# Two more units of a convolution moved to channel-major jobs, with neighbouring blocks sharing a job

## The chip, the cores and the metric

The kernel runs on one core of a Trainium2 chip. The metric is the device time of one execution in microseconds (us). A core has five engines that run side by side and wait for one another by semaphores: TensorE (PE, matrix products; its weight loads are listed as PEld), VectorE (DVE), ScalarE (ACT), GpSimd (POOL) and SyncE (SP, which here only issues DMAs). DMAs are issued from SP's queue or from POOL's and carried out by 16 DMA engines. Each engine works through its own instructions in program order.

## The reference

A causal convolution with one softmaxed filter of 7 taps for each of 8 groups of 24 channels, and then a gated feed-forward block, both over 8 sequences of 4096 tokens with 192 channels:

```python
w = softmax(weight)                      # 8 groups x 7 taps
x_pad = concatenate([zeros((B, 6, D)), x], axis=1)
out = einsum('hk,bskhg->bshg', w, windows of x_pad)   # 24 channels of a group share the 7 taps
x = out.reshape(32768, 192)
g = x @ w_gate                           # 192 x 1536
silu = g * (1.0 / (1.0 + exp(-g)))
val = x @ w_val
return (silu * val) @ w_out              # 1536 x 192
```

## The kernel before

**Tiling.** The 32768 tokens are 64 blocks of 512 (`TB`), four blocks to a unit (`UT` = 2048 tokens, 16 units, two to a sequence). The feed-forward part walks over the blocks; the 1536 inner features are 12 chunks of 128, so a block has 12 steps, a unit 48 (`ustep`), the kernel 768. The main loop at line 892 runs over steps n; b is the block, j the chunk, u the unit, ls the step in the unit.

**A step.** `gate_val` issues six matmuls of 64 x 128 weights on 512 columns (line 772), three channel tiles k for gate and val each, in pairs that run side by side in two halves of the PE array. ACT makes silu of the gate (line 781), DVE multiplies it with val (line 783). PSUM has three buffers each for gate and val. At j = 1, 4, 7 and 10 a `slot` follows, with the down projection's matmuls (line 798), and after the last of them the copies and the DMA of a block's output (lines 856 to 860).

**The input of a block** is three tiles of 128 channels x 512 tokens in fp16: channels 0 to 127, 64 to 191, and 128 to 191 with 0 to 63 (gate reads one half of a tile, val the other). There are two ways to make them:

- *On PE.* Units 0 (by a variant of its own for its four blocks), 1, 3, 7 and 11. x is loaded token-major by a DMA from POOL (`load_x`), doubled by SP (`dup_x`), multiplied with a band matrix on PE in two halves (`conv_half`, at ls 10 and 22 of the unit before), copied out of PSUM by ACT and DVE, completed by a copy on POOL (`conv_dup`), stored to DRAM by nine DMAs (`conv_out`) and read back by DMA transposes (`fetch`), three to a block.
- *Channel-major.* The units in `POOLED` (line 53): 2, 4, 5, 6, 8, 9, 10, 12 to 15. `cast_x` copies a unit of x to DRAM in fp16 (a DMA from POOL, line 590); `turn_x` reads it back transposed (line 605), so that channels lie on partitions and a tap is a shift along the tokens. There are two such tiles for each block, channels 0 to 127 (`x01`) and 64 to 191 (`x12`). Channels 128 to 191 fill only half the partitions, so those of two blocks share a tile: `join_x` (line 609) moves one block's 64 rows to the free half of another's. A unit then has six jobs (`conv_job`): four "block" jobs for channels 0 to 127, two "pair" jobs for 128 to 191. A job is, in order: two products on ACT (line 680; tap 0 into `total`, tap 3 into `part`), two multiply-adds on DVE (line 655, taps 1 and 2), and on POOL one add of `part` and, for taps 4, 5 and 6, a product (line 645) and an add (line 630) each. `total` has five buffers. The last add writes `pxc0` of the block, or `y2` of the pair. `place` then builds the other two tiles with four DMAs from SP (line 704).

**What sets the order.** `planned(v)` writes down the step of each piece for a channel-major unit v whose first step is s0 = 48 v: the cast at s0 - 112, the ten transposes and joins from s0 - 105, two steps apart, and the jobs into the lists at s0 - 89. Unit 2 has times of its own. `pooled_work` runs in each step: at j = 1, 7 and 10 it takes one DVE piece and one ACT piece off their lists (unless a `conv_half` or an early convolution runs in this step), which makes 12 turns in a unit, as many as a unit has pieces. POOL's seven instructions of a job are written when its ACT and DVE pieces are. `place` for block i is written when both its jobs are, at least 18 steps later (14 in unit 2), and not before s0 + 12 i - 16. All these instructions go to the queue of their engine in the order written, so a DMA that waits in SP's queue holds up those behind it, and a cast stands in POOL's queue behind the jobs written before it.

Of the kernel before, what the change touches and what calls it, by code (L numbers as in the profile page):

```python
# [10 lines left out]
def kernel(  # L11
# [9 lines left out]
    nc = tc.nc  # L21
# [13 lines left out]
    P = 128  # L35
    Q = 64
# [13 lines left out]
    ER = ((0, 3), (3, 5))  # L50
    XW = 2 * EG * EO
    NU = NT // UT
    POOLED = (2, 4, 5, 6, 8, 9, 10, 12, 13, 14, 15)
    upb = S // UT
    n_blocks = NT // TB
    n_steps = n_blocks * NCH
# [16 lines left out]
    def seq(i):  # L73

        e = i.ins.engine
        if e in last_on:
            tc.add_manual_dep(i.ins, last_on[e].name, NOSYNC, reason="order")
        last_on[e] = i.ins
        return i
# [106 lines left out]
    def small(name, shape, dt=fp32):  # L186
        return wpool.tile(shape, dt, tag=name, name=name)
# [106 lines left out]
    tap = small("tap", [P, 2 * H], fp16)  # L294
# [249 lines left out]
    x12 = {}  # L544
    y2 = {}
    taps = {}
# [29 lines left out]
    def cast_x(u):  # L576
        rows = XP + UT
        xs[u] = dpool.tile([rows, D], fp16, tag="xs", name="xs")
        flat = xs[u].rearrange("t d -> (t d)")
        skip = XP if u % upb == 0 else 0  # L580
        if skip:
            seq(
                nc.sync.dma_start(
                    out=flat[0 : XP * D].rearrange("(a n) -> a n", n=P),
                    in_=fill[0 : XP * D // P, :],
                )
            )
        n = (rows - skip) * D // P
        seq(
            nc.gpsimd.dma_start(  # L590
                out=flat[skip * D : rows * D].rearrange("(a n) -> a n", n=n),
                in_=bass.AP(
                    tensor=x_flat.tensor,
                    offset=(u * UT - XP + skip) * D,
                    ap=[[n, P], [1, n]],
                ),
            )
        )

    def turn_x(u, i, at):  # L600
        rows = xs[u][TB * i : TB * i + TB + XP]
        tiles = (x01, x12)[at // Q]
        tag = f"x{at // Q}"
        t = cpool.tile([P, TB + XP], fp16, tag=tag, name=tag, bufs=8)
        seq(nc.sync.dma_start_transpose(out=t, in_=rows[:, at : at + P]))
        tiles[u, i] = t

    def join_x(u, i):
        seq(nc.sync.dma_start(out=x12[u, i + 2][0:Q], in_=x12[u, i][Q:P]))

    FIRST, ON_DVE, ON_ACT, ON_POOL = 0, (1, 2), (3,), (4, 5, 6)
    act_steps = []
# [5 lines left out]
    def conv_job(u, what, i):  # L618
        index = n_jobs[0]
        n_jobs[0] += 1  # L620
        job = {"dve": len(ON_DVE), "act": len(ON_ACT), "parts": []}
        at = XP - pad

        def shifted(k):
            return job["src"][:, at + k : at + k + TB]

        def add(part, k):
            total = job["total"]
            seq(
                nc.gpsimd.tensor_tensor(  # L630
                    job["dst"] if k == K - 1 else total, total, part, op=ALU.add
                )
            )

        def proceed():
            if job["dve"]:
                return
            while job["parts"]:
                add(*job["parts"].pop(0))
            if job["act"]:  # L640
                return
            for k in ON_POOL:
                part = cpool.tile([P, TB], fp32, tag="piece", name="piece", bufs=2)
                seq(
                    nc.gpsimd.tensor_scalar(  # L645
                        part, shifted(k), scalar1=job["tap"][:, k : k + 1],
                        scalar2=1.0, op0=ALU.mult, op1=ALU.mult,
                    )
                )
                add(part, k)  # L650
            finished[u, what, i] = step_now[0]

        def dve_step(k):
            seq(
                nc.vector.scalar_tensor_tensor(  # L655
                    job["total"], shifted(k), job["tap"][:, k : k + 1], job["total"],
                    op0=ALU.mult, op1=ALU.add,
                )
            )
            job["dve"] -= 1  # L660
            proceed()

        def act_step(k):
            if k == FIRST:
                if what == "pair":
                    y2[u, i] = cpool.tile([P, TB], fp16, tag="y2", name="y2", bufs=4)
                    job.update(dst=y2[u, i], src=x12[u, i + 2], tap=taps["c2"])
                else:
                    t = cpool.tile([P, XW], fp16, tag="pxc0", name="pxc0", bufs=8)
                    xc[UB * u + i] = [t]  # L670
                    job.update(dst=t[:, 0:TB], src=x01[u, i], tap=taps["c01"])
                part = job["total"] = cpool.tile(
                    [P, TB], fp32, tag="total", name="total", bufs=5
                )
                dve_steps.extend((index, lambda k=k: dve_step(k)) for k in ON_DVE)
            else:
                part = cpool.tile([P, TB], fp32, tag="part", name="part", bufs=6)
                job["parts"].append((part, k))
            seq(
                nc.scalar.activation(  # L680
                    part, shifted(k), AF.Copy, scale=job["tap"][:, k : k + 1]
                )
            )
            if k != FIRST:
                job["act"] -= 1
                proceed()

        act_steps.extend((index, lambda k=k: act_step(k)) for k in (FIRST, *ON_ACT))

    def place(u, i):  # L690
        b = UB * u + i
        for k in (1, 2):
            xc[b].append(
                cpool.tile([P, XW], fp16, tag=f"pxc{k}", name=f"pxc{k}", bufs=4)
            )
        t0, t1, t2 = xc[b]
        y = y2[u, i % 2][Q * (i // 2) : Q * (i // 2) + Q, :]
        for dst, src in (
            (t1[0:Q, 0:TB], t0[Q:P, 0:TB]),
            (t1[Q:P, 0:TB], y),  # L700
            (t2[0:Q, 0:TB], y),
            (t2[Q:P, 0:TB], t0[0:Q, 0:TB]),
        ):
            seq(nc.sync.dma_start(out=dst, in_=src))  # L704

    def pooled(u):
        return u in POOLED

# [2 lines left out]

    def queue_jobs(u):
        for job in (
            ("block", 0), ("pair", 0), ("block", 1), ("pair", 1),
            ("block", 2), ("block", 3),
        ):
            conv_job(u, *job)
        placing.extend((u, i) for i in range(UB))

    def planned(v):  # L720
        s0 = ustep * v
        turns = (
            (0, 0), (0, Q), (2, Q), None, (1, 0), (1, Q), (3, Q), None, (2, 0), (3, 0)
        )
        if v == 2:
            cast, jobs = 21, 55
            times = (36, 36, 36, 38, 39, 39, 39, 41, 43, 43)
        else:
            cast, jobs = s0 - 112, s0 - 89
            times = range(cast + 7, cast + 27, 2)  # L730
        plan.setdefault(cast, []).append(lambda: cast_x(v))
        for m, turn in enumerate(turns):
            if turn:
                todo = lambda turn=turn: turn_x(v, *turn)
            else:
                todo = lambda i=m // 4: join_x(v, i)
            plan.setdefault(times[m], []).append(todo)
        plan.setdefault(jobs, []).append(lambda: queue_jobs(v))

    def pooled_work(n, j, busy):  # L740
        step_now[0] = n
        if not busy:
            ready = dve_steps[0][0] if dve_steps else None
            ahead = act_steps[0][0] if act_steps else n_jobs[0]
            if j in (1, 7, 10) and ready is not None:
                dve_steps.pop(0)[1]()
            if j in (1, 7, 10) and act_steps and (ready is None or ahead < ready + 3):
                act_steps.pop(0)[1]()
        while placing:
            u, i = placing[0]  # L750
            need = (u, "block", i), (u, "pair", i % 2)
            if not all(job in finished for job in need):
                break
            done = max(finished[job] for job in need)
            if n < max(done + (14 if u == 2 else 18), ustep * u + NCH * i - 16):
                break
            placing.pop(0)
            place(u, i)
# [129 lines left out]
    make_band()  # L888
    for v in POOLED:
        planned(v)  # L890

    for n in range(n_steps):
        b, j = divmod(n, NCH)
        u, ls = divmod(n, ustep)
# [31 lines left out]
        if n == 37:  # L926
            make_channel_taps()
        pooled_work(n, j, work is not None)
        if u + 1 < NU and not pooled(u + 1):
            if ls == at[0]:  # L930
# [62 lines left out]
```

## Time and profile before

| what | us |
|---|---|
| median of 3 runs (lowest, highest) | 784.47 (784.04, 785.72) |
| the profiled execution, whole | 786.03 |
| its span in the profile | 784.3 |
| PE busy | 774.7 |
| weight loads busy | 631.6 |
| DVE busy | 675.1 |
| ACT busy | 584.7 |
| POOL busy | 551.1 |

Three groups of instructions make up nearly all of POOL's time: 264 adds of line 630, of 1.32 to 1.37 us each, and 198 products of line 645 of 0.83. POOL's busy share in 40 equal slices of the span (a digit is tenths, 9 is 90% or more) shows where it works:

```profile
POOL 9100797699999990089999996029999999996000
```

Its three long stretches belong to the jobs of units 4 to 6, 8 to 10 and 12 to 15; the stretch of unit 2 is the shorter one ahead of them. Matmuls overlap, so a busy PE is not PE at its peak. Idle time of an engine that nobody waits for costs nothing; what counts is which wait ends last at a place where PE stands still.

### The profile page before, as it was taken

How to read it: one execution, taken by the hardware profiler on the slowest of the kernel's cores; microseconds unless marked ns; L12 is line 12 of the kernel's file. 1: busy time of each engine (PE TensorE's matmuls, PEld its weight loads, DVE VectorE, ACT ScalarE, POOL GpSimd, SP SyncE). 2: the span in 40 equal slices, each digit the busy share in tenths (PEclk: the TensorE clock that was granted, in tenths of full speed). 3: DMA queues.
4: the chain of work that ended last, by engine and by line, in shares of the span. 5: the costliest groups of instructions: out<-in, count | busy, mean ns of one | idle time of the engine just before them, and what ended most of it. 6: DMA issues, size and time to landing. Idle time of an engine off the chain costs nothing.

```text
span 784.3 us, 27860 instructions
## 1 busy us (share of the span) xinstructions
PE 774.7 (99%) x11307; PEld 631.6 (81%) x11307; DVE 675.1 (86%) x1018; ACT 584.7 (75%) x999; POOL 551.1 (70%) x523
## 2 busy tenths in 40 slices
PE   8999998999999999999999999999999999999997
PEld 5666675688888888778888888868989988888886
DVE  6686996999999987799999997789999999997775
ACT  6576885788788766787787776687787787876664
POOL 9100797699999990089999996029999999996000
PEclk9999998999999999999999999999999999999999
DMA  9949753675551296585364239557635255221211
GB/s 140 179 116 144 167 104 95 125 104 117 111 124 45 60 166 113 113 141 101 101 114 93 69 70 175 120 129 106 130 80 125 76 100 109 69 62 42 69 56 42
DMA packets 154470, 82.37 MB, mean 105 GB/s; under 512 B 98110, under 2 KB 153798, under 8 KB 153798
## 3 DMA queue, kind: packets, MB, share of 16 engines
q1 hardware_dynamic: 136422, 64.26, 37.4%
q0 software_dynamic: 17920, 16.34, 14.5%
q8 instruction: 88, 1.44, 0.8%
q14 instruction: 40, 0.33, 0.1%
HBM read 32.68 MB, written 38.34 MB: 91 GB/s over the span
## 4 chain that ended last, share of the span: by engine, by line
PE 96%; POOL 2%; ACT 0%; DVE 0%; DMA 0%; issue 0%; SPq 0%; POOLq 0%
PE val L772 36%; PE acc L798 31%; PE gate L772 27%; POOL total L630 1%; PE warm L873 1%; POOL piece L645 1%; PE cv L476 1%; PE turn L445 0%; PE cv L387 0%; PE acc L819 0%; DVE h L783 0%; DMA pxc<-pxc 0%; SPq L704 0%; POOL y L630 0%; ACT sig L781 0%
## 5 line engine op out<-in xcount | busy, mean ns | idle before, releaser
L781 ACT ACTIVATE sig<-gate 128x512 f16<-128x512 f32 x768 | 458.6, 597 | 181.9 <-PE gate L772 122.4
L783 DVE TENSOR_TENSOR h<-sig,val 128x512 f16<-128x512 f16 x768 | 502.5, 685 | 98.4 <-PE gate L772 65.0
L772 PEld LDWEIGHTS <-w 64*128 64x128 f16 x4608 | 362.4, 110 | 111.5 <-issue 6.8
L772 PE MATMUL gate<-pxc,w 64*128 64x512 f16 x1584 | 373.4, 377 | 2.3 <-DMA pxc<-pxc 2.2
L772 PE MATMUL val<-pxc,w 64*128 64x512 f16 x1584 | 373.0, 377 | 0.1
L798 PE MATMUL acc<-wo,h 64*128 64x192 f16 x6096 | 327.3, 243 | 0.6 <-issue 0.5
L798 PEld LDWEIGHTS <-h 64*128 64x128 f16 x6096 | 301.5, 94 | 27.5 <-issue 2.9
L630 POOL TENSOR_TENSOR total<-total,piece 128x512 f32<-128x512 f32 x132 | 179.1, 1357 | 11.0
L772 PE MATMUL gate<-xc,w 64*128 64x512 f16 x720 | 169.7, 376 | 0.0
L772 PE MATMUL val<-xc,w 64*128 64x512 f16 x720 | 169.6, 376 | 0.1
L645 POOL TENSOR_SCALAR piece<-x,both_taps 128x512 f32<-128x512 f16 x198 | 164.2, 829 | 0.0
L655 DVE SCALAR_TENSOR_TENSOR total<-x,both_taps,total 128x512 f32<-128x512 f16 x132 | 138.7, 1051 | 0.0
L630 POOL TENSOR_TENSOR total<-total,part 128x512 f32<-128x512 f32 x66 | 90.4, 1369 | 59.1 <-DVE total L655 58.1
L630 POOL TENSOR_TENSOR pxc<-total,piece 128x512 f16<-128x512 f32 x44 | 58.2, 1322 | 3.7
L504 POOL COPY tm<-tm 128x1280 f16<-128x1280 f16 x4 | 5.0, 1250 | 67.0 <-DVE tm L493 67.0
L680 ACT ACTIVATE part<-x,both_taps 128x512 f32<-128x512 f16 x66 | 47.1, 714 | 0.0
L680 ACT ACTIVATE total<-x,both_taps 128x512 f32<-128x512 f16 x66 | 47.1, 714 | 0.0
L857 DVE COPY o_sb<-acc 128x384 f32<-128x384 f32 x63 | 34.6, 549 | 0.0
L630 POOL TENSOR_TENSOR y<-total,piece 128x512 f16<-128x512 f32 x22 | 29.5, 1341 | 1.8
L856 ACT COPY o_sb<-acc 128x384 f32<-128x384 f32 x63 | 30.3, 481 | 0.1
L98 POOL DMA_DIRECT2D x<-in_x_dram x10 | 8.7, 885 | 24.4 <-ACT sig L781 24.4
L493 ACT CAST tm<-cv 128x480 f16<-128x480 f32 x16 | 8.2, 562 | 5.8 <-PE cv L476 5.8
(67 smaller groups left out, 85.9 us busy)
## 6 DMA issues: line engine op xcount, KB each, us to landing
out_dram<-o_sb SPq DMA_DIRECT2D x63, 384.0 KB
pxc<-pxc SPq DMA_DIRECT2D x88, 64.0 KB
pxc<-y SPq DMA_DIRECT2D x88, 64.0 KB
xs<-in_x_dram POOLq DMA_DIRECT2D x7, 768.0 KB, 6.9
x<-in_x_dram POOLq DMA_DIRECT2D x10, 480.0 KB, 9.3
scr<-tm SPq DMA_DIRECT2D x28, 130.0 KB
xs<-in_x_dram POOLq DMA_DIRECT2D x4, 774.0 KB, 8.9
x<-x SPq DMA_DIRECT2D x6, 480.0 KB
```

What stands on the lines that cost most here:

```text
L98: nc.gpsimd.dma_start(out=t[p0 + i0 : p0 + i1, w0 - at : w1 - at, :], in_=bass.AP(tensor=x_flat.tensor, offset=(t0 + size * w0 - pad + i0) ...
L493: eng(tm[u][:, NG * r : NG * r + NG, 2 * grp * hp : 2 * grp * hp + 2 * grp].rearrange("p g (t e) -> p g t e", t=2), banks[r][:, 0 : 2 * w] ...
L630: nc.gpsimd.tensor_tensor(job["dst"] if k == K - 1 else total, total, part, op=ALU.add)
L645: nc.gpsimd.tensor_scalar(part, shifted(k), scalar1=job["tap"][:, k : k + 1], scalar2=1.0, op0=ALU.mult, op1=ALU.mult,)
L655: nc.vector.scalar_tensor_tensor(job["total"], shifted(k), job["tap"][:, k : k + 1], job["total"], op0=ALU.mult, op1=ALU.add,)
L680: nc.scalar.activation(part, shifted(k), AF.Copy, scale=job["tap"][:, k : k + 1])
L772: nc.tensor.matmul(o, w16[m][p0 : p0 + Q, k, e::E], xc[b][k][p0 : p0 + Q, 0:TB], start=(k == 0), stop=(k == SL - 1),)
L781: silu[n] = seq(nc.scalar.activation(sg, g, AF.Silu)).ins
L783: seq(nc.vector.tensor_tensor(hj, sg, v, op=ALU.mult))
L798: nc.tensor.matmul(acc[b][bank][:, s, :], hj[p0 : p0 + Q, ts(2 * bank + s, P)], wo16[p0 : p0 + Q, j, :], start=(not second and j == 0 and ...
L856: seq(nc.scalar.copy(o_sb[:, 0:2, :], acc[b][0]))
L857: seq(nc.vector.tensor_copy(o_sb[:, 2:4, :], acc[b][1]))
```

## The change

`POOLED` takes in every unit from 4 on, so units 7 and 11 are made channel-major too, and only units 1 and 3 are still made on PE (unit 0 keeps its variant). A pair job now joins blocks 0 and 1, or 2 and 3, instead of 0 and 2, or 1 and 3. The order of the jobs and of the transposes follows: block 1 needs three jobs ahead of its placing instead of four. Unit 4's cast and transposes are written 12 steps later (its jobs are not); in unit 2 one transpose and the order of the others change.

```diff
-    POOLED = (2, 4, 5, 6, 8, 9, 10, 12, 13, 14, 15)
+    POOLED = (2, *range(4, NU))
...
     def join_x(u, i):
-        seq(nc.sync.dma_start(out=x12[u, i + 2][0:Q], in_=x12[u, i][Q:P]))
+        seq(nc.sync.dma_start(out=x12[u, 2 * i + 1][0:Q], in_=x12[u, 2 * i][Q:P]))
...
-                    job.update(dst=y2[u, i], src=x12[u, i + 2], tap=taps["c2"])
+                    job.update(dst=y2[u, i], src=x12[u, 2 * i + 1], tap=taps["c2"])
...
-        y = y2[u, i % 2][Q * (i // 2) : Q * (i // 2) + Q, :]
+        y = y2[u, i // 2][Q * (i % 2) : Q * (i % 2) + Q, :]
...
     def queue_jobs(u):
         for job in (
-            ("block", 0), ("pair", 0), ("block", 1), ("pair", 1),
-            ("block", 2), ("block", 3),
+            ("block", 0), ("pair", 0), ("block", 1),
+            ("block", 2), ("pair", 1), ("block", 3),
         ):
...
         turns = (
-            (0, 0), (0, Q), (2, Q), None, (1, 0), (1, Q), (3, Q), None, (2, 0), (3, 0)
+            (0, 0), (0, Q), (1, Q), None, (1, 0), (2, 0), (2, Q), (3, Q), None, (3, 0)
         )
         if v == 2:
             cast, jobs = 21, 55
-            times = (36, 36, 36, 38, 39, 39, 39, 41, 43, 43)
+            times = (36, 36, 36, 38, 39, 39, 41, 41, 43, 43)
         else:
-            cast, jobs = s0 - 112, s0 - 89
+            late = 12 if v == 4 else 0
+            cast, jobs = s0 - 112 + late, s0 - 89
             times = range(cast + 7, cast + 27, 2)
...
-                todo = lambda i=m // 4: join_x(v, i)
+                todo = lambda i=m // 8: join_x(v, i)
...
-            need = (u, "block", i), (u, "pair", i % 2)
+            need = (u, "block", i), (u, "pair", i // 2)
```

## The prediction

> **What bounds the kernel now.** I read the chain of waits first, then the windows by unit, then the timelines of POOL, SP and PE. The chain says that TensorE (PE) carries nearly everything:
>
> ```profile
> PE 96%; POOL 2%; ACT 0%; DVE 0%; DMA 0%; issue 0%; SPq 0%; POOLq 0%
> ```
>
> The few per cent of POOL in it are one place, where unit 2, the first channel-major unit, begins its second block. The chain in order of time, cut to 90 to 150 us, and PE's timeline there:
>
> ```profile
> 122.60 0.68 POOL piece L645
> 123.28 0.89 SPq L704
> ...
> 124.85 2.05 DMA pxc<-pxc
> ```
> ```profile
> 125.33 0.37 PE L772 MATMUL gate<-pxc,w 64*128 64x512 f16 x1 [2.21 <-DMA pxc<-pxc]
> ...
> 127.32 0.63 PE L772 MATMUL val<-pxc,w 64*128 64x512 f16 x1
> ```
>
> PE stood 2.2 us, and its matmuls then took 0.63 instead of 0.38 us until 132.2. A steady block of 12 steps takes 11.73 us (0.9775 a step); between the L798 groups at 96.25 and 151.32 lie 48 steps, which should take 46.92 and took 55.07. Of the surplus 8.15, 1.4 is the convolution of unit 3 on PE (below), so the stall cost 6.7.
>
> The windows, one per unit (columns: span, then busy time of PE, weight loads, DVE, ACT, POOL, clock, DMA), show the second resource at its limit:
>
> ```profile
> 384.50:431.40 46.90, 46.90 (x676) 41.08 (x673) 44.69 (x65) 37.81 (x65) 45.46 (x42) 1.00 0.49 101
> ...
> 478.30:525.30 47.00, 47.00 (x727) 37.05 (x724) 35.94 (x57) 32.99 (x57) 8.55 (x9) 1.00 0.57 128
> ```
>
> A channel-major unit issues 43 POOL instructions (six jobs of seven, one cast DMA), and POOL ends only 42 in the 46.93 us that PE needs for a unit: it falls behind. In the second window, around unit 11, it rests and catches up. POOL's timeline gives its pace:
>
> ```profile
> 573.28 1.27 POOL L630 TENSOR_TENSOR total<-total,part 128x512 f32<-128x512 f32 x1
> ...
> 622.27 1.72 POOL L630 TENSOR_TENSOR total<-total,part 128x512 f32<-128x512 f32 x1
> ...
> 630.95 0.56 POOL L590 DMA_DIRECT2D xs<-in_x_dram  x1
> ```
>
> The first lines are the first adds of units 13 and 14: 48.99 us a unit. Units 5 to 6 (195.06 to 244.05) and 9 to 10 (384.17 to 433.17) give 48.99 and 49.00; 14 to 15 gives 49.90. So POOL loses 2.06 us a unit. Taken against the end of the job's second L655 on DVE, the lag at the first jobs of units 12 to 15 is 0.16, 3.11, 5.15 and 7.61 us.
>
> Where lag hurts is SP. The cast of unit 15 stands in POOL's queue behind the jobs of unit 14; SP's first transpose (L605) waits for it, and behind that in SP's queue stand the placing DMAs (L704) of unit 13:
>
> ```profile
> 637.57 1.13 SPq L605 DMA_TRANSPOSE x<-xs  x1
> 638.80 0.52 SPq L860 DMA_DIRECT2D out_dram<-o_sb  x1
> 639.38 3.25 SPq L605 DMA_TRANSPOSE x<-xs  x2
> 642.74 0.52 SPq L704 DMA_DIRECT2D pxc<-pxc  x1
> 643.39 1.16 SPq L704 DMA_DIRECT2D pxc<-y  x2
> 644.92 0.46 SPq L704 DMA_DIRECT2D pxc<-pxc  x1
> ```
> ```profile
> 649.51 0.38 PE L772 MATMUL gate<-pxc,w 64*128 64x512 f16 x1
> ```
>
> The cast at 630.95 lands at 637.57 (6.62 later). The fourth placing DMA is issued by 645.38 and lands some 2.05 later (the chain's DMA piece above), at 647.4. The matmul at 649.51 is the first that needs it (step 636, block 1 of unit 13, third channel tile). So 2.1 us of margin are left. Relative to PE's time at the step where each cast is written (steps 512, 560, 608, counted back from 649.08 at 0.9775), the casts of units 13, 14, 15 are 3.25, 6.5 and 9.2 us late: the margin is gone at 11.3.
>
> [...] L645 takes 0.69 us in some places and 1.13 in others[...], and a whole job takes 7.36 us after DVE's last L655 (712.45 to 719.81) and (48.99 - 0.57)/6 = 8.07 on average.
>
> **The change, part by part.**
> *Units 7 and 11 leave the PE convolution.* Removed per unit: 64 matmuls, 8 evictions, the dup, two load DMAs on POOL, 9 stores and 12 fetch transposes on SP. On PE: from the L798 group at 303.89 to that at 352.24 lie 48 steps, 48.35 against 46.92, so 1.4 us a unit, gain 2.8. The other engines' removed work is hidden now and gives nothing.
> *They join the channel-major units.* Added per unit: 12 L680 on ACT (0.71 each), 12 L655 on DVE (1.05), 42 POOL instructions and a cast, 8 transposes, 2 joins, 16 placing DMAs. ACT and DVE hold: full units show 37.8 and 44.7 of 46.9 us with no wait on POOL. On SP about as much goes as comes. POOL is the cost: units 4 to 15 are now twelve in a row, where before at most four were, so it never catches up.
> *Sum along POOL's queue.* First add of unit 5 at 195.06; nine units of 48.99 bring the first add of unit 14 to 635.97; from there to the cast of unit 15 8.68 as now, 644.65. Once PE itself is held to POOL's pace, DVE disturbs it less per us: (8.07-7.36) x 6 = 4.3 us a unit, times 48.99/46.93 - 1, is 0.2, over seven units 1.3: 643.35. Minus the gain in unit 2 (next part, 1.0): 642.35. Landing 6.62, transposes and placing 9.86 (637.57 to 647.43): the matmul that stood at 649.51 can't start before 658.8. Without any wait it would come at 649.51 - 2.8 - 1.0 = 645.7. So PE must stand 13.1 us in all, about 1.9 at the second block of each of units 7 to 13 (the casts of 9 to 15, the fifth channel-major unit in a row being just at the limit). The join order leaves this chain as it is: before the placing still stand three transposes.
> *Three jobs and later transposes, in unit 2.* POOL now ends block 1's job second in turn after the first pair, at 108.3 instead of 108.9, and its placing stands in front of unit 4's transposes: ready by 113, far before it is needed at 122.9. The 6.7 us go. But unit 4's cast now stands behind four jobs: 83.75, 91.96, 100.19, 108.3, so at 116.4, landed at 123.1. SP stands until then. Behind it: five transposes (1.28), an output DMA, a join that waits some 1.5, then block 2's placing, at 132.4, fully landed at 137.0, against a need at 122.75 + 11.73 + 0.65 + 0.43 = 135.6: 1.4 us late. Then three transposes, a join, an output, the nine stores of unit 3 (5.7, as at 141.41 to 147.08) and block 3's placing at 146.3 to 147.2, landed at 150.8 to 151.8, against a need at 135.56 + 1.4 + 11.73 = 148.7: 2 to 3 us late. Before, that matmul ran at 153.72. So the gain is 2 to 3 us[...]; I take 1.0, ends -1.5 and +4 (if SP is quicker and neither wait comes). The ACT job of unit 4 that first reads a transposed tile (step 109, about 124.8) waits some 1.2 us; three PSUM buffers of gate cover that, else it costs the same 1.2.
> *Clock after the late stalls.* Unseen for short stalls: between 0 and the 4.5 us that the stall of unit 2 cost beyond its 2.2 of idling. It doesn't add up, since POOL catches up meanwhile; only what outlasts the last one counts. I take 1.3, about a third.
>
> End: 658.8 + 1.3 - 649.5 = +10.6 on the span of 784.3, 794.9. That execution took 786.03, span and 1.7 around it, and the three runs have a median of 784.47; I put the same difference on the median: 795.1 us.
>
> **Rivals.**
> A, faster: POOL's jobs shorten as their phase against DVE drifts, and the lag stays harmless. The point of decision: the stalls must stay under the 3.8 gained, so 13.1 - 9 x (48.99 - X) = 3.8, X = 47.96 a unit, 7.90 us a job. For it: jobs of 7.6 occur. Against: four full stretches repeat 49.0, one is longer. Time without stalls 784.47 - 3.8 = 780.7. Chance 0.04.
> B, the limit sits later: SP's order isn't what PE meets; the next ring is the five "total" buffers that ACT fills. There ACT's first product has 14.0 us in hand in unit 15 (four in a row), 2.07 less a unit: none at the eleventh, a wait of 2. Time 784.47 - 3.8 + 2 = 782.7. Against: the 2.1 us margin on SP is a read number. Chance 0.03.
> C, clock: the last stalls each end in a slow stretch and unit 2 gains nothing: 795.1 - 1.3 + 4.5 + 2.5 = 800.8. For: 2.2 us were enough once. Against: stalls of 1.9 may be too short. Chance 0.13.
>
> **How the numbers follow.** Forecast 0.80, C 0.13, A 0.04, B 0.03. A measurement of this kernel tells about 0.2% (1.6 us) from no change. POOL's pace within 0.3 us a unit moves the end by 2.7 either way, unit 2 by +2.5 or -3, the clock by -1.3 or +3.2. The range 788.5 to 800.5 takes these in. Faster: A and B, 0.07; the same: the tail between them and the forecast, 0.02; slower: 0.91.
>
> **What would show it.** POOL busy from about 140 to beyond 700 us with no pause at units 7 and 11; the casts later by some 2 us a unit until about unit 9, then at a steady lateness near 11; waits of PE's L772 on DMA pxc of 10 to 14 us in total, at block 1 of units 7 to 13; the cast of unit 15 near 643; the wait in unit 2 moved from block 1 to blocks 2 and 3. Jobs under 7.9 us, or no wait on pxc after unit 6, would make it wrong.

## The result, and the profile after

The changed kernel takes 809.56 us (median of 4 runs, 809.28 to 810.5), the one before 784.25 in the same series: 1.0321 times as long, 95% interval 1.0303 to 1.0339. The span of the profiled execution is 808.7 us against 784.3. The direction was as predicted; the size was not, 809.6 against 795.1 and a range that ended at 800.5.

The page of the changed kernel, POOL's busy share by slices and the shares of the chain that ended last:

```profile
POOL 9000896659999999999999999999999999998000
...
PE 75%; POOL 14%; issue 4%; DMA 3%; SPq 1%; DVE 1%; ACT 1%; POOLq 0%; DVEq 0%
```

POOL works without a pause from slice 10 to slice 36; the two rests are gone, and PE's share of the chain fell from 96 to 75%. (The change adds one line, so that L773 and L784 here are L772 and L783 of the kernel before.) The lag of POOL's first add behind the end of the job's second L655 on DVE, for the first jobs of units 4 to 9, is 0.14, 1.87, 3.90, 6.25, 10.05 and 10.04 us, and it then stays between 4.4 and 12.1: it is held. Where it is held shows in the timelines of POOL, SP and PE at the last cast:

```profile
656.50 0.56 POOL L590 DMA_DIRECT2D xs<-in_x_dram  x1
```
```profile
663.50 1.15 SPq L605 DMA_TRANSPOSE x<-xs  x1
664.75 0.52 SPq L861 DMA_DIRECT2D out_dram<-o_sb  x1
665.33 3.00 SPq L605 DMA_TRANSPOSE x<-xs  x2
668.43 0.52 SPq L704 DMA_DIRECT2D pxc<-pxc  x1
669.00 2.06 SPq L704 DMA_DIRECT2D pxc<-y  x2
671.11 0.59 SPq L704 DMA_DIRECT2D pxc<-pxc  x1
```
```profile
671.28 0.37 PE L773 MATMUL gate<-pxc,w 64*128 64x512 f16 x1 [1.24 <-DMA pxc<-pxc]
...
672.56 0.58 PE L773 MATMUL gate<-pxc,w 64*128 64x512 f16 x1 [0.30 <-DMA pxc<-y]
```

It is the same chain as in the kernel before, link by link, but now PE waits at its end. The recorded waits on placing DMAs from unit 7 on add up to 7.9 us, at block 1 of units 7, 8, 9, 11, 12 and 13 and at block 2 of some of these; the largest is 2.3 us, in unit 9. There the matmuls then ran at 0.58 to 0.63 us until 481 (granted clock 0.50 from 474.74 to 481.2), so that PE fell back by some 6 us at once, and unit 10 had no wait.

The other surprise sits in unit 2. PE's timeline there:

```profile
136.31 0.37 PE L773 MATMUL gate<-pxc,w 64*128 64x512 f16 x1 [0.48 <-DMA pxc<-pxc]
...
157.65 0.58 PE L773 MATMUL gate<-pxc,w 64*128 64x512 f16 x1 [8.44 <-DMA pxc<-pxc]
```

The 2.2 us at block 1 are gone, block 2 is late by two waits of less than 0.5 us, and at block 3 PE stands 8.4 us, after which its matmuls take 0.58 to 0.63 us until about 164 (granted clock 0.50 from 157.65 to 163.5). SP's timeline says why block 3 is late:

```profile
138.04 1.36 SPq L605 DMA_TRANSPOSE x<-xs  x1
142.87 0.47 SPq L609 DMA_DIRECT2D x<-x  x1
143.38 1.27 SPq L605 DMA_TRANSPOSE x<-xs  x1
144.75 5.45 SPq L512 DMA_DIRECT2D scr<-tm  x8
150.25 2.36 SPq L520 DMA_DIRECT2D scr<-tm  x1
152.71 2.65 SPq L704 DMA_DIRECT2D pxc<-pxc  x1
155.41 1.37 SPq L704 DMA_DIRECT2D pxc<-y  x2
156.82 0.60 SPq L704 DMA_DIRECT2D pxc<-pxc  x1
```

Two things are late here. SP stands from 139.40 to 142.87, until the transposed tile that the join moves has landed. And the ninth store took 2.36 us to issue and the first placing DMA 2.65, where the kernel before shows 0.37 and 0.47:

```profile
146.71 0.37 SPq L520 DMA_DIRECT2D scr<-tm  x1
147.19 0.47 SPq L704 DMA_DIRECT2D pxc<-pxc  x1
```

While the eight stores ahead of them are being issued, POOL issues unit 5's cast, 774 KB:

```profile
148.29 0.57 POOL L590 DMA_DIRECT2D xs<-in_x_dram  x1
```

### The profile page after: what moved, and what is told of

Same layout as the page of the kernel before. It is cut to its first block, busy times and chain, and to the rows that moved or that the text cites. A ratio compares the mean times of both kernels' runs of the same rounds, so it can differ in the third digit from the quotient of the medians.

```text
span 808.7 us, 27812 instructions
## 1 busy us (share of the span) xinstructions
PE 783.5 (97%) x11179; PEld 596.2 (74%) x11179; DVE 698.8 (86%) x1034; ACT 596.5 (74%) x1015; POOL 645.2 (80%) x603
## 4 chain that ended last, share of the span: by engine, by line
PE 75%; POOL 14%; issue 4%; DMA 3%; SPq 1%; DVE 1%; ACT 1%; POOLq 0%; DVEq 0%
PE val L773 34%; PE acc L799 24%; PE gate L773 14%; POOL total L630 6%; POOL piece L645 6%; DMA pxc<-pxc 2%; POOL pxc L630 1%; DMA pxc<-y 1%; SPq L704 1%; POOL y L630 1%; DVE h L784 1%; PE warm L874 1%; ACT sig L782 0%; DMA x<-xs 0%; SPq L605 0%
## 5 line engine op out<-in xcount | busy, mean ns | idle before, releaser
L784 DVE TENSOR_TENSOR h<-sig,val 128x512 f16<-128x512 f16 x768 | 500.5, 684 | 99.9 <-PE gate L773 42.1
L773 PEld LDWEIGHTS <-w 64*128 64x128 f16 x4608 | 338.0, 110 | 169.7 <-issue 33.6
L773 PE MATMUL gate<-pxc,w 64*128 64x512 f16 x1872 | 447.4, 379 | 13.8 <-DMA pxc<-pxc 12.5
L773 PE MATMUL val<-pxc,w 64*128 64x512 f16 x1872 | 444.9, 378 | 3.9 <-DMA pxc<-pxc 2.2
L630 POOL TENSOR_TENSOR total<-total,piece 128x512 f32<-128x512 f32 x156 | 205.9, 1320 | 13.0
L645 POOL TENSOR_SCALAR piece<-x,both_taps 128x512 f32<-128x512 f16 x234 | 206.3, 882 | 0.0
L655 DVE SCALAR_TENSOR_TENSOR total<-x,both_taps,total 128x512 f32<-128x512 f16 x156 | 173.5, 1112 | 0.0
L630 POOL TENSOR_TENSOR total<-total,part 128x512 f32<-128x512 f32 x78 | 104.2, 1336 | 35.2 <-DVE total L655 34.9
L773 PE MATMUL val<-xc,w 64*128 64x512 f16 x432 | 102.0, 376 | 0.8 <-DVE h L784 0.7
L773 PE MATMUL gate<-xc,w 64*128 64x512 f16 x432 | 102.2, 376 | 0.0
L630 POOL TENSOR_TENSOR pxc<-total,piece 128x512 f16<-128x512 f32 x52 | 70.2, 1349 | 4.3
```

What stands on the lines that cost most here:

```text
L630: nc.gpsimd.tensor_tensor(job["dst"] if k == K - 1 else total, total, part, op=ALU.add)
L645: nc.gpsimd.tensor_scalar(part, shifted(k), scalar1=job["tap"][:, k : k + 1], scalar2=1.0, op0=ALU.mult, op1=ALU.mult,)
L655: nc.vector.scalar_tensor_tensor(job["total"], shifted(k), job["tap"][:, k : k + 1], job["total"], op0=ALU.mult, op1=ALU.add,)
L773: nc.tensor.matmul(o, w16[m][p0 : p0 + Q, k, e::E], xc[b][k][p0 : p0 + Q, 0:TB], start=(k == 0), stop=(k == SL - 1),)
L784: seq(nc.vector.tensor_tensor(hj, sg, v, op=ALU.mult))
```

## The experiments

**1. Unit 4's transposes at their old steps.** All twelve units from 4 on stay channel-major.

```diff
-            late = 12 if v == 4 else 0
+            late = 0
```

> The changed kernel with unit 4's cast and transposes at their old steps (late = 0). Theory: the cast that stands behind four jobs held SP, unit 2's block 3 came late, and PE is 7.2 us behind the kernel before at step 145 where without any stall it would be 6.7 us ahead: the stall is worth 13.9 us, and POOL's queue carries it to the end. So 795.7 us, ratio to before 1.0145, no L773 wait on DMA pxc in unit 2, first add of unit 5 near 188. Rival: the stall in unit 2 is made good later, since the late units wait for POOL's pace anyhow: within 3 us of the changed kernel's 809.6.

Measured: 795.37 us, ratio 1.0147 (1.0132 to 1.0162). At step 145, in unit 4's fourth job, DVE ends its L655 at 162.2 instead of 175.9, 13.8 us earlier, and the end comes 14.2 earlier: nothing of unit 2's loss is made good later. The waits of PE on these DMAs (total, times, longest), first the changed kernel, then this one:

```profile
PE gate L773 <- DMA pxc<-pxc: 12.5, 4, 8.4
```
```profile
PE gate L773 <- DMA pxc<-pxc: 3.1, 3, 1.1
```

The first wait on a placing DMA in this kernel is at 324 us, at block 2 of unit 6; none is in unit 2. What remains, 11.3 us over before, is POOL's pace less what unit 2 gains here (6.6 us) and PE saves in units 6 and 10; against experiment 8, where nobody waits for POOL, it is 17.0.

**2. Units 7 and 11 back on PE, unit 4 still late.**

```diff
-    POOLED = (2, *range(4, NU))
+    POOLED = (2, 4, 5, 6, 8, 9, 10, 12, 13, 14, 15)
```

> The changed kernel with units 7 and 11 back on PE (POOLED as before); the new pairs, the new order of the jobs and unit 4's later cast stay. Theory: POOL gets its two rests back and its lag stays under the margin of SP's queue, so only the loss of unit 2 is left: before + 7.2, 791.4 us, ratio 1.009. Rival: the slow part comes from the new job and transpose order itself, not from twelve units in a row: above 800 us.

Measured: 794.40 us, ratio 1.0130 (1.0115 to 1.0146). PE's one large wait is again block 3 of unit 2:

```profile
157.84 0.58 PE L773 MATMUL gate<-pxc,w 64*128 64x512 f16 x1 [9.56 <-DMA pxc<-pxc]
```

At step 145 it is 7.4 us behind the kernel before, at unit 8 and at unit 15 8.8, so nothing is lost after unit 7. The 1.4 between those places is for the most part (0.9) one step in unit 3. DVE there starts an L655 while POOL issues unit 6's cast, and PE waits 0.69 us for the product of line 784 behind it:

```profile
210.68 0.55 POOL L590 DMA_DIRECT2D xs<-in_x_dram  x1
```
```profile
210.84 2.42 DVE L655 SCALAR_TENSOR_TENSOR total<-x,both_taps,total 128x512 f32<-128x512 f16 x1
```

The changed kernel has the same (2.43 us, at 210.59). The median is 3 above what was expected: 1.6 of that shows in the profile (8.8 where 7.2 was counted on), and the rest comes from the profiled execution of the kernel before, which at 786.03 was 2 us above its median in this series, so that the difference from it is too small.

**3. Both undone: only the pairs and the orders.** `late = 0` and `POOLED` as before.

> The new pairs and orders alone: POOLED as before, late = 0. Theory: block 1 of unit 2 waits for three jobs and stands in front of most of unit 4's transposes in SP's queue, the old stall of 6.7 us goes and nothing replaces it: 777.6 us, ratio 0.9915. Rival: another wait takes its place in unit 2 (block 2 or 3): 782 to 785 us.

Measured: 779.76 us, ratio 0.9945 (0.9928 to 0.9961), faster than before, though by 4.3 and not 6.7 us; the profiled spans differ by 6.2 (778.1 against 784.3), since that profiled execution of the kernel before was one of its longer ones. Against experiment 2 only `late` differs, and that is worth 14.6 us, as in experiment 1. The chain's shares:

```profile
PE 99%; DVE 0%; ACT 0%; issue 0%
```

POOL and the placing are out of it: the three jobs do what their words say, and no other wait takes the place.

**4. The casts taken out of the lag.** As experiment 1, and each cast from unit 5 on is written 24 steps earlier. POOL has the same instructions to do.

```diff
-        plan.setdefault(cast, []).append(lambda: cast_x(v))
+        plan.setdefault(cast - (24 if v > 4 else 0), []).append(lambda: cast_x(v))
```

> As the kernel with late = 0 and twelve channel-major units in a row from unit 4 on, but each cast after unit 4's is written 24 steps earlier, so that it is not behind the lag in POOL's queue when SP's first transpose wants it. POOL does exactly the same work. Theory: the lag reaches PE through SP's queue (cast, transposes, placing in order); with this cut the lag grows on past 12 us and PE first meets the five total buffers near unit 14: 776 to 781 us, POOL lag above 18 us in unit 14. Rival: PE is held to POOL's pace in any case (by ACT's buffers or by DVE), whatever SP's order: 793 to 797 us, lag again flat near 10 to 12.

Measured: 785.67 us, ratio 1.0013 (1.0004 to 1.0022), between the two. PE has no wait on the placing DMAs left, and the lag grows freely, to 12.2 us at unit 8 and 23.5 at unit 12; so SP's order was what held PE. But the next ring came sooner than I thought. ACT's waits in this kernel, and one of them in its timeline:

```profile
ACT total L680 <- POOL pxc L630: 14.6, 12, 2.5
```
```profile
564.12 0.72 ACT L680 ACTIVATE total<-x,both_taps 128x512 f32<-128x512 f16 x1 [1.97 <-POOL pxc L630]
```

From unit 12 on ACT's first product starts 0.04 us after POOL gives a `total` buffer back. The reason is the pace: from unit 5 to 12 POOL takes 50.0 us a unit (189.39 to 539.44), not 49.0, so the five buffers ran out two units earlier; against experiment 8, which has eight, that cost 7.3 us in all.

**5. DVE's taps left out from unit 8 on.** As experiment 1; taps 1 and 2 are missing in the output of units 8 to 15.

```diff
         def dve_step(k):
-            seq(
...
+            if u < 8:
+                seq(
...
             job["dve"] -= 1
```

> As the kernel with late = 0, but DVE's two multiply-adds (taps 1 and 2, line 655) are left out in units 8 to 15, so those two taps are missing in the output. POOL's instructions are the same. Theory: POOL's pace is its own 0.69 and 1.27 us an instruction plus what an L655 running beside it adds; without L655 a job takes 7.36 us, a unit 44.7, less than PE's 46.93, the lag of 10 at unit 8 melts away within some five units and PE waits no more after about unit 8: 776 to 780 us. Rival: the pace is POOL's own or comes from DVE's other work (line 783): jobs stay near 8.1 us and the time near 795.

Measured: 778.31 us (a single run). POOL's groups between 400 and 690 us (count, busy, mean ns), first of the changed kernel, then of this one:

```profile
L645 POOL TENSOR_SCALAR piece<-x,both_taps 128x512 f32<-128x512 f16 x105 | 95.0, 904 | 0.0
...
L630 POOL TENSOR_TENSOR pxc<-total,piece 128x512 f16<-128x512 f32 x24 | 32.6, 1360 | 2.0
```
```profile
L645 POOL TENSOR_SCALAR piece<-x,both_taps 128x512 f32<-128x512 f16 x114 | 79.0, 693 | 0.0
...
L630 POOL TENSOR_TENSOR pxc<-total,piece 128x512 f16<-128x512 f32 x26 | 33.1, 1272 | 2.2
```

Without L655 a job starts every 7.30 us, a unit takes 44.4, and PE's last wait on a placing DMA is at 372 us. DVE's other work (the product of line 784) runs on, and with it POOL's instructions take no longer than alone: 0.693 and 1.27 us on average.

**6. One product of the pair jobs moved from POOL to ACT.** As experiment 1.

```diff
+    ON_ACT_TOO = ("pair",)
...
-            for k in ON_POOL:
+            for k in ON_POOL[1 if what in ON_ACT_TOO else 0 :]:
...
-                part = cpool.tile([P, TB], fp32, tag="part", name="part", bufs=6)
+                part = cpool.tile([P, TB], fp32, tag="part", name="part", bufs=8)
...
+            if k != FIRST and what in ON_ACT_TOO:
+                k2 = ON_POOL[0]
+                part = cpool.tile([P, TB], fp32, tag="part", name="part", bufs=8)
+                job["parts"].append((part, k2))
+                seq(
...
```

> As the kernel with late = 0, with tap 4's product of the two pair jobs of each unit made on ACT in the turn of tap 3 instead of on POOL (its add stays on POOL; the part ring grows to 8). Theory: POOL's unit falls by two products of 0.7 to 1.0 us from 49.5 to about 47.8, the lag grows by 0.9 us a unit instead of 2.5 and reaches the margin of SP's queue only at the end: 776 to 781 us. Rival: ACT's two longer turns a unit hold up silu and PE: above 785.

Measured: 783.38 us, ratio 1.0020 (0.9993 to 1.0047), twelve runs from 781.2 to 783.5 and eight from 788.6 to 792.1: no difference from the kernel before is shown. The profile is of one of the shorter runs. In the profile POOL's unit is 48.03 us (casts at 243.98 and, eight units on, at 628.22), near the 47.8 expected, and PE waits on placing DMAs again from 548 us on, the longest for 0.7. The pace came out as expected, the time 2 us above the expected range; why the runs fall into two groups some 9 us apart was not tried.

**7. Unit 5's cast behind one more job.** The changed kernel, with that cast and its transposes 3 steps later.

```diff
-            late = 12 if v == 4 else 0
+            late = {4: 12, 5: 3}.get(v, 0)
```

> The changed kernel (unit 4 late) with unit 5's cast and transposes written 3 steps later, so that in POOL's queue the cast stands behind unit 4's first pair job. It was issued at 148.3 and moved 774 KB in the very time in which unit 3's nine stores and the placing of unit 2's block 3 were in SP's queue. Theory: that traffic is what made the placing 5 us later than I had summed (SP reached it at 152.7, not 147.2): the wait of 8.4 us falls to about 5, and the end to 805.5. Rival: the stores and transposes in SP's own queue did it: wait 8 or more, time 809 to 811.

Measured: 803.74 us, ratio 1.0251 (1.0223 to 1.0280), 5.8 us below the changed kernel. SP's and PE's timelines:

```profile
144.57 5.84 SPq L512 DMA_DIRECT2D scr<-tm  x8
150.46 0.36 SPq L520 DMA_DIRECT2D scr<-tm  x1
150.92 0.47 SPq L704 DMA_DIRECT2D pxc<-pxc  x1
151.43 1.23 SPq L704 DMA_DIRECT2D pxc<-y  x2
152.71 0.60 SPq L704 DMA_DIRECT2D pxc<-pxc  x1
```
```profile
152.89 0.37 PE L773 MATMUL gate<-pxc,w 64*128 64x512 f16 x1 [4.13 <-DMA pxc<-pxc]
```

With the 774 KB out of the way the ninth store and the placing issue as fast as in the kernel before, and the wait falls from 8.4 to 4.1 us. SP still comes to the stores at 144.6, some 4 us later than my sum had it (nine stores of 5.7 us before a placing at 146.3): the join in front waited for its transpose until 142.7 here too. Of the 5.8 us, 3.9 are unit 2's (first add of unit 5 at 198.36 against 202.26); the rest came later, where the next nine units took 444.3 against 446.2.

**8. Eight buffers for `total`.** As experiment 4.

```diff
-                    [P, TB], fp32, tag="total", name="total", bufs=5
+                    [P, TB], fp32, tag="total", name="total", bufs=8
...
-                part = cpool.tile([P, TB], fp32, tag="part", name="part", bufs=6)
+                part = cpool.tile([P, TB], fp32, tag="part", name="part", bufs=7)
```

> As the kernel with late = 0 and the casts 24 steps earlier, with eight total buffers instead of five (and seven parts instead of six). POOL's work is unchanged. Theory: the five buffers were the next limit (ACT's first product found its buffer free only 0.04 us before from unit 12 on); three more give 23.5 us, the lag grows past 30 us and nothing waits: 776 to 779 us. Rival: another hold of POOL's (the transposed tiles, y2, the placing) takes over at once: 783 to 786.

Measured: 778.36 us, ratio 0.9921 (0.9902 to 0.9940), the lowest median of the kernels whose output is whole, 7.3 us below experiment 4. The lag reaches 30.6 us at unit 15, with POOL as slow as ever (nine units from the cast at 172.48 to that at 622.08, 49.96 each), and nobody waits for it. The chain's shares:

```profile
PE 96%; SPq 1%; DMA 1%; DVE 0%; ACT 0%; issue 0%
```

So a POOL that is 3 us a unit too slow for PE is no loss by itself, for as long as the buffers outlast the kernel.

## Why the prediction was wrong in size

Link by link along the chain that the prediction summed, predicted and measured in the profiled executions:

| link | predicted us | measured us | off |
|---|---|---|---|
| first add of unit 5 | 194.1 | 202.26 | +8.2 |
| nine units, to the first add of unit 14 | 439.6 | 446.20 | +6.6 |
| from there to the cast of unit 15 | 8.68 | 8.04 | -0.6 |
| cast to the matmul that waits for it | 16.5 | 16.06 | -0.4 |
| that matmul to the end of the span | 136.1 | 136.1 | 0 |
| span | 794.9 | 808.7 | +13.8 |

The two ends of that second link, in the timeline of the changed kernel's POOL:

```profile
202.26 1.27 POOL L630 TENSOR_TENSOR total<-total,part 128x512 f32<-128x512 f32 x1
...
648.46 1.26 POOL L630 TENSOR_TENSOR total<-total,part 128x512 f32<-128x512 f32 x1
```

**Right.** POOL's queue sets the end, through cast, transposes and placing in SP's queue; the margin of 11.3 us (counted back from the matmul that waits, the last cast is 11.7 late) and the last two links came out as written. The waits came from unit 7 on at block 1, but unit 10 had none, there were some at block 2, and they add up to 7.9 us where 10 to 14 were forecast. Experiment 4 shows that it is this order, and experiment 8 that with more buffers for the next ring as well the slow POOL costs nothing. Rivals A and B are out: jobs got longer, not shorter, and the ring of `total` comes second. C, the clock after the last stalls, is out too: the missing 14 us are in the first two links of the table, though PE fell back by a further 2.7 us of the first link while its matmuls were slow after the stall of 8.4 (that stretch of granted clock 0.50). The saving on PE is there (units 6 and 10, in which the convolutions of 7 and 11 ran, took 48.35 us before and 46.92 now), but net experiment 8 is only 1.4 us below experiment 3, not 2.8; where the rest goes was not traced.

**Wrong, first term: "block 3's placing at 146.3 to 147.2, landed at 150.8 to 151.8", and from it a gain of 1.0 in unit 2 (the sum gave 2 to 3, and 1.0 was my estimate).** The order in SP's queue was right, the durations were not. The sum had the second join wait for nothing; it stood 3.5 us for its tile, so that SP came to the stores at 144.75 instead of some 140.6. And the nine stores and the placing were priced as in the kernel before, where SP had stood idle ahead of them (from 135.65 to 141.41). Here they follow the transposes at once, and unit 5's cast, which I had left where it was, comes 4.6 us earlier (148.29 against 152.91) because PE does, into the same window. SP got to the placing at 152.7, it was all issued at 157.4, and unit 2 lost 7.2 us instead of gaining 1.0. Experiment 7 gives the share of unit 5's cast, 3.9 us in unit 2; experiment 1 gives all of it, 14.2 at the end between this stall and none. That the later cast and transposes of unit 4 are the cause is shown. The error was to price the DMAs behind them at the issue times of a quiet queue, and to leave out a wait. The price of a cast beside a placing stood in the trace of the kernel before, 1.3 us behind the issue of unit 4's cast (100.14):

```profile
101.40 3.07 SPq L704 DMA_DIRECT2D pxc<-pxc  x1
```

**Wrong, second term: "nine units of 48.99", less 1.3 for an eased DVE.** The pace isn't a constant of POOL. In the changed kernel's timeline, DVE and POOL side by side:

```profile
648.74 1.54 DVE L655 SCALAR_TENSOR_TENSOR total<-x,both_taps,total 128x512 f32<-128x512 f16 x1
649.71 1.13 POOL L645 TENSOR_SCALAR piece<-x,both_taps 128x512 f32<-128x512 f16 x1
...
652.17 0.69 POOL L645 TENSOR_SCALAR piece<-x,both_taps 128x512 f32<-128x512 f16 x1
```

Sorted by whether an L655 runs beside it (for more than some 0.1 us), a product takes 0.69 us alone and 1.05 with one, an add 1.27 and about 1.4 (all of the changed kernel's). Before, 87 of 198 products had one beside them; now 126 of 234. What that adds to a unit can be summed from the durations. Over the 44.4 us that a unit takes without L655, the units of 49.0 before have 2.2 us more in products and 2.4 in adds; units 8 and 9 of the changed kernel (49.6) have 4.6 and 0.6; most of experiment 8's (50.0) 3.2 and 2.4. So the nine units took 49.58 us each on average, and some 50.0 in experiments 4 and 8, where the lag went on to 24 and 31. Experiment 5 shows that what a unit takes above 44.4 is L655's doing. My correction had the wrong sign: I let the disturbance thin out with PE's pace, where it grew with the lag. That the phase of the jobs against DVE makes it grow, rather than lag by some other way, is argued from these counts and was not tried by itself. A sign of it was on record. Three stretches of the kernel before repeat 49.0, not four as the prediction has it, and the one with the largest lag, unit 14 to 15, took 49.90; the sum took 48.99 for all nine. Experiment 1 holds this term alone: with its gain in unit 2 (6.6 instead of 1.0) the forecast's sum would give 789.5, and it took 795.37. That this is also about where the forecast for the changed kernel stood is chance.

The clock term, 1.3 us, was about right: the last link took 134.8 us before and 136.1 now, with a granted clock of 0.54 from 672.56 to 676.

## What to carry to other kernels

A margin between queues is read from the trace before the change: the last consumer's start less the landing of what it waits for, and how much of it each further unit eats. An engine that falls behind by 2 or 3 us a unit is harmless while the slack of its buffers and of the queue orders behind it lasts, and sets the pace from there on; from experiment 1, moving what waits behind it in an in-order queue brought 9.7 us and more buffers another 7.3, with POOL no faster; lightening it by one product in each pair job alone brought 12.0. A transfer that is moved is priced at the queue it moves into, with what else lands there once everything around it comes earlier.

## What the runs showed of the hardware

- POOL's products and adds are lengthened by L655 when it runs beside them, from 0.69 to 1.05 us and from 1.27 to about 1.4 in the changed kernel; with L655 left out, and the product of line 784 running on, they take 0.693 and 1.27 (experiment 5). DVE pays too: L655 takes 0.75 us where POOL is idle (at 77.48 before) and 1.05 on average.
- The longest L655 of the changed kernel (2.43 us, at 210.59) started while POOL issued a cast, as one of 2.42 in experiment 2 did (at 210.84), and the longest before (2.13, at 278.69) while POOL issued two loads of x; another beside two loads took 1.05 (at 467.79 before). The three that started 0.08 to 0.13 us behind a cast of the changed kernel took 1.90 to 1.95, and no other there more than 1.85.
- A cast of 774 KB from POOL's queue held up SP's issue of small DMAs: 0.36 and 0.47 us without it (experiment 7) became 2.36 and 2.65. In the kernel before, a placing DMA took 3.07 us to issue behind unit 4's cast (at 101.40), and the one that ends the placing of the next block 0.60 (at 124.85).
- SP issued its DMAs in the order written: in the changed kernel none from 643.99 until the last cast had landed at 663.50, and the placing of unit 13's block 1 came at 668.43, behind three transposes, though POOL had ended unit 13's jobs by 648.5.
- Slow matmuls came without a long pause: after waits of 1.24, 0.24 and 0.30 us at 671 to 672 us in the changed kernel a matmul took 0.58 instead of 0.37, and the granted clock was 0.54 from 672.56 to 676. But three waits of 0.21, 0.26 and 0.33 us at 423 to 424.5 had no slow matmul behind them, at a granted clock of 1.00.
